# Second MoE in units of 256 tokens with four banks per layer, maxima turned by TensorE, weight sums in the first MoE's last span

## The chip, the cores and the metric

The program runs on one core of one Trainium2 chip. The metric is the device time of one execution in microseconds (us). Five engines matter: PE (TensorE matmul, with PEld its weight loads), DVE (VectorE), ACT (ScalarE), POOL (GpSimd) and SP (SyncE), which issues most DMAs. Accumulators live in PSUM, which the kernel uses as eight banks of 128 x 512 f32; everything else on the chip is in SBUF.

## The reference, cut to what matters

```python
def reference(q, k, v, s, moe_w_in, moe_w_out, moe2_w_in, moe2_w_out):
    a = _attn_ref(q, k, v, s)              # 4 batches, 8 heads, 576 tokens, 64 per head
    x = a.transpose(0, 2, 1, 3).reshape(2304, 512)
    x = _moe_ref(x, moe_w_in, moe_w_out)
    return _moe2_ref(x, moe2_w_in, moe2_w_out)

def _moe_ref(x, w_in, w_out):              # first MoE
    h = x @ w_in                           # 2304 x 512 by 512 x 2048
    sp = np.where(h > 20.0, h, np.log1p(np.exp(np.minimum(h, 20.0))))
    return (h * np.tanh(sp)) @ w_out       # 2304 x 2048 by 2048 x 512

def _moe2_ref(x, w_in, w_out):             # second MoE
    h = x @ w_in
    return (h * (1.0 / (1.0 + np.exp(-1.702 * h)))) @ w_out
```

## The kernel before

Every f32 product is made from three matmuls: each operand is split into a high and a low part, and `mm3` issues high by high, high by low and low by high into one accumulator (three code lines, L593 to L595). The program has three stages. The first holds the attention and the first layer of the first MoE, and ends with the hidden values in DRAM (`h_d`). The second is the second layer of the first MoE. The third is the second MoE.

**Tokens.** The 2304 tokens are cut into five spans, four of 512 and one of 256. Both later stages go span by span.

**Second layer of the first MoE (the loop over `groups1`, L922 on).** Per span, PE accumulates 16 blocks of 128 hidden rows into the span's accumulators: four banks of `acc` for 512 tokens, two for 256, taken with `bank()` in rotation from two pools of eight banks in all. After each block, `bg_step()` runs one background job: conversion and maxima of the second MoE's weights (`out_pass1`, which leaves the output weights in DRAM as `w2_d`, `in_pass`, `in_split`, and the two scales `out_scale` and `in_scale`). At the end of a span ACT copies the accumulators to SBUF (`x2`, L948), DVE takes maxima of absolute values (L823), they go to DRAM (`x2_d`), and a last reduce (L953) leaves one maximum per partition. `across` then takes the maximum over the 128 partitions: a DMA writes the column to a row in DRAM (`row_d`, L790), a second reads the row back to all partitions (L792), and DVE reduces it (L793). It is called seven times, for five spans and for the two weight scales. Behind it on DVE stand the scale computations (`span_scale`).

**Second MoE.** `prep_x(u)` reads a span's `x2_d` and splits it to f16 (ACT L915, DVE L916). `first2` makes one bank of the first layer (`h`): for a span of 512 it is 12 matmuls of 512 columns, twice for each of eight indices j; for the span of 256 it is 24 matmuls of 256 columns, once per j. The pool `ps_1` has one bank for all of this. ACT takes the sigmoid from the bank (L118), DVE multiplies (`z`, L1007). The second layer has Strassen's form with seven products instead of eight: `combos` builds the four sums of blocks of z on POOL (L1015 to L1018) and splits z and the sums into high and low parts (`gh`, `gl`, L1021, L1022); `second2` accumulates the seven products (`p`), one bank each (`ps_7`, seven banks). `pend` holds the second-layer work back by a few steps (`LGH = 4`). `finish` evacuates the seven products into the output rows.

**Weight sums.** `out_pass2(j)` makes the seven block sums of the output weights for pair j: two reads of `w2_d` (`w2f`), four POOL subtractions (`w2d`, L970), three ACT copies (`w2h`, L979) and three DVE subtractions (`w2l`, L980). In the program two of the eight calls stand ahead of the second MoE and six in its first span.

**What sets the order.** The kernel is written in a framework with a scheduler that fixes a static order on every engine when the program is built. Each engine runs its list in order, so an instruction that waits holds back all behind it on that engine.

Of the kernel before, what the change touches and what calls it, by code (L numbers as in the profile page):

```python
# [28 lines left out]
LGH = 4  # L29
# [25 lines left out]
def attention_moe_moe_kernel(  # L55
# [34 lines left out]
    row_d = dram.tile([16, 128], F32, name="row_d")  # L90
# [694 lines left out]
    row_n = [0]  # L785
# [49 lines left out]
    def out_scale():  # L835
        amax(gsc[:, 0:1], wom)
        across(gsc[:, 0:1])
# [32 lines left out]
    def in_scale():  # L870
        nc.vector.tensor_reduce(out=gsc[:, 2:3], in_=rk[:, :, 1], axis=mybir.AxisListType.X, op=ALU.max)
        across(gsc[:, 2:3])
# [47 lines left out]

    acc1 = {}
    for i, (u, t0, W, m0, n) in enumerate(groups1):  # L922
# [8 lines left out]
        for j in range(n):  # L931
# [9 lines left out]
            bg_step()  # L941
        if m0 + n == NF:
# [11 lines left out]
            across(spx[:, u, 0:1])  # L954
            if ready[0]:
                span_scale(u)
            else:
                waiting.append(u)
    while bg:
        bg_step()  # L960

    w2o_t = {}

    def out_pass2(j):
        y = wst_b.tile([128, 2, 512], F32, tag="wst", name="w2f", bufs=NRAW)
        for e in range(2):
            nc.sync.dma_start(out=y[:, e, :], in_=w2_d[j + NF // 2 * e])
        d = tmp_pair(F32, "w2d").rearrange("p (s f) -> p s f", s=4)
        b11, b12, b21, b22 = (y[:, e, h * 256:(h + 1) * 256] for e in range(2) for h in range(2))
        sub = lambda o, a, b_: nc.gpsimd.tensor_tensor(out=o, in0=a, in1=b_, op=ALU.subtract)  # L970
        sub(d[:, 0], b12, b11)
        sub(d[:, 2], b22, b12)
        sub(d[:, 1], b22, d[:, 0])
        sub(d[:, 3], d[:, 1], b21)
        th, tl_ = (wb_p.tile([128, 7, 256], F16, tag="w", name=nm) for nm in ("w2h", "w2l"))
        k = gsc[:, 0:1]
        for s0, s1, src in ((0, 1, y[:, 0, 0:256]), (1, 3, y[:, 1, :]), (3, 7, d.rearrange("p s f -> p (s f)"))):
            h, l = (x[:, s0:s1, :].rearrange("p s f -> p (s f)") for x in (th, tl_))
            nc.scalar.activation(out=h, in_=src, func=AF.Copy, scale=k)  # L979
            nc.vector.scalar_tensor_tensor(out=l, in0=src, scalar=k, in1=h, op0=ALU.mult, op1=ALU.subtract)  # L980
        w2o_t[j] = th, tl_
# [4 lines left out]
    ps_1 = enter_b(tc.tile_pool(name="ps_1", bufs=1, space=PSUM, reuse_waits="tile"))  # L986
# [3 lines left out]
    SECOND = ((6, 2, 5), (4, 0, 3), (2, 3, 2), (3, 5, 6))  # L990
    prod = {}
    ev = {}
    pend = []
    NP = NF // 2

    def first2(u, j, W, e, z, sg):
        ps = ps_1.tile([128, 512], F32, tag="h", name="h2")
        ms = [(0, j + NP if e == 0 else j)] if W == 512 else [(0, j + NP), (1, j)]
        x = x16[u]
        for d, m in ms:  # L1000
            o = ps[:, d * W:(d + 1) * W]
            for c in range(KC):
                t = w2t[c, m // 8]
                hi, lo = (t[:, a, m % 8 * 128:m % 8 * 128 + 128] for a in range(2))
                mm3(o, hi, lo, x[:, 0, c, 0:W], x[:, 1, c, 0:W], d == 0 and c == 0, c == KC - 1)
# [3 lines left out]
    def combos(z, hb):  # L1009
        q_ = z[:, 0:4 * hb].rearrange("p (s t) -> p s t", s=4)  # L1010
        a12, a22, a11, a21 = (q_[:, k] for k in range(4))
        st = tmp_pair(F32, "s2")[:, 0:4 * hb]
        sv = st.rearrange("p (s t) -> p s t", s=4)
        tt = nc.gpsimd.tensor_tensor
        tt(out=sv[:, 0], in0=a21, in1=a22, op=ALU.add)  # L1015
        tt(out=sv[:, 2], in0=a11, in1=a21, op=ALU.subtract)
        tt(out=sv[:, 1], in0=sv[:, 0], in1=a11, op=ALU.subtract)
        tt(out=sv[:, 3], in0=a12, in1=sv[:, 1], op=ALU.subtract)  # L1018
        h, l = (wa_p.tile([128, 7 * 256], F16, tag="w", name=nm)[:, 0:7 * hb] for nm in ("gh2", "gl2"))
        for s0, n_, src in ((4 * hb, 3 * hb, z[:, 0:3 * hb]), (0, 4 * hb, st)):  # L1020
            nc.scalar.activation(out=h[:, s0:s0 + n_], in_=src, func=AF.Copy)  # L1021
            nc.vector.tensor_tensor(out=l[:, s0:s0 + n_], in0=src, in1=h[:, s0:s0 + n_], op=ALU.subtract)  # L1022
        return h, l

    def second2(u, j, hb, which, h, l):
        nt = hb // 128
        if j == 0:
            for p, _, _ in which:
                prod[u, p] = ps_7.tile([128, 512], F32, tag=f"p{p}", name=f"p{p}")
        th, tl_ = w2o_t[j]  # L1030
        for p, a, b_ in which:
            for tb in range(nt):
                o = prod[u, p][:, tb * 256:(tb + 1) * 256]
                ts = slice(a * hb + tb * 128, a * hb + (tb + 1) * 128)
                mm3(o, h[:, ts], l[:, ts], th[:, b_], tl_[:, b_], j == 0 and tb == 0, j == NP - 1)

    def finish(u, W, part):
        t0 = spans[u][0]
        nt = W // 256
        n_ = nt * 256  # L1040
        k, nk = spx[:, u, 3:4], spx[:, u, 0:1]
        pv = lambda p: prod[u, p][:, 0:n_].rearrange("p (t f) -> p t f", t=nt)
# [4 lines left out]
        def tmp(nm):  # L1047
            t = mb.tile([128, 512], F32, tag="x2", name=nm, bufs=4)
            return t[:, 0:n_].rearrange("p (t f) -> p t f", t=nt)

        if part == 0:
            ev[u, "lo"], ev[u, "hi"] = lo, hi = [
                wst_b.tile([128, 2, 512], F32, tag="wst", name=nm, bufs=NRAW)[:, 0:nt] for nm in ("olo", "ohi")
            ]
            e1 = tmp("e1")
            nc.scalar.activation(out=e1, in_=pv(0), func=AF.Copy, scale=k)
            add(lo[:, :, 0:256], 1, e1)
            ev[u, "u2"] = tmp("u2")
            add(ev[u, "u2"], 5, e1)
        else:  # L1060
            lo, hi, u2 = (ev.pop((u, x)) for x in ("lo", "hi", "u2"))
            u3, u4 = tmp("u3"), tmp("u4")
            add(u3, 6, u2)
            add(u4, 4, u2)
            add(hi[:, :, 256:512], 4, u3)
            add(lo[:, :, 256:512], 2, u4)
            add(hi[:, :, 0:256], 3, u3, nk)
            for half, o in enumerate((lo, hi)):
                r0 = t0 + half * W // 2
                nc.sync.dma_start(out=out[r0:r0 + W // 2, :].rearrange("(t p) f -> p t f", p=128), in_=o)  # L1070

    def push(u, j, W, z):
        hb = W // 2
        h, l = combos(z, hb)
        for part, which in enumerate((FIRST, SECOND)):
            def go(part=part, which=which):
# [57 lines left out]
```

## Time and profile before

| What | us |
| --- | --- |
| Median of 3 runs (lowest, highest) | 1088.12 (1085.77, 1090.79) |
| The profiled execution, its own time | 1082.65 |
| Its span in the profile | 1080.8 |
| PE busy in the span | 964.4 (89%) |
| DVE, ACT, POOL busy | 686.2, 562.9, 389.2 |
| First MoE's second layer on PE | 452 to 663 |
| Second MoE on PE, first to last matmul | 662.9 to 1075.1 |

Times in the trace count from the start of the span. The profiled execution is 5.47 us below the median of the runs, and 1.85 us of it lie outside its span. Matmuls are pipelined: the listed length of one is longer than the distance from one start to the next, and the distance is what a sequence costs.

### The profile page before, as it was taken

Reading aid. Unit: us, or ns where it says so; the run is one execution under the profiler, and the core shown is the slowest. Engines: PE = TensorE matmul, PEld = TensorE weight load, DVE = VectorE, ACT = ScalarE, POOL = GpSimd, SP = SyncE. Lnnn points to the kernel's source line nnn. Section 1 sums busy time; section 2 is a strip of 40 time slices with the busy share of each in tenths; the row PEclk is TensorE's granted clock in tenths of the full one; section 3 lists DMA queues with packets and bytes.
Section 4 is the critical chain, followed back from the end, with each engine's and each line's share of the span. In section 5 each row is a group of like instructions: output and inputs, shape, how many; then the busy total and the mean of one; then the engine's idle time right before and its main releaser. Section 6 shows DMA issues by size and latency. Waiting matters only on the chain.

```text
span 1080.8 us, 18613 instructions
## 1 busy us (share of the span) xinstructions
PE 964.4 (89%) x7044; PEld 776.8 (72%) x7044; DVE 686.2 (63%) x1266; ACT 562.9 (52%) x1078; POOL 389.2 (36%) x434
## 2 busy tenths in 40 slices
PE   5587799999999999999999986399989999998997
PEld 4476698888888889988887875156656565665686
DVE  5897776575567756999877945535643553463454
ACT  4886777585658863565555545234333423332332
POOL 3454532241223114772211316155332423333343
PEclk7788999999999999999999997599999999999999
DMA  9799997996799898899894656100110010010010
GB/s 238 175 224 265 243 221 160 211 207 175 162 204 206 153 171 262 282 354 317 266 265 149 234 106 136 61 1 1 39 40 1 3 57 2 1 39 1 1 40 20
DMA packets 185865, 153.87 MB, mean 142 GB/s; under 512 B 118896, under 2 KB 154096, under 8 KB 185776
## 3 DMA queue, kind: packets, MB, share of 16 engines
q1 hardware_dynamic: 179744, 135.38, 50.3%
q0 software_dynamic: 6032, 17.31, 6.8%
q8 instruction: 55, 0.90, 0.3%
q14 instruction: 34, 0.28, 0.1%
HBM read 93.86 MB, written 32.58 MB: 117 GB/s over the span
## 4 chain that ended last, share of the span: by engine, by line
PE 31%; DMA 16%; DVE 12%; issue 5%; ACT 4%; POOL 3%; SPq 0%; DVEq 0%; POOLq 0%; ACTq 0%
PE h L593 6%; PE h L594 6%; PE h L595 6%; PE p L595 4%; PE p L593 4%; PE p L594 4%; DMA row_d<-spx 4%; DMA bc<-row_d 3%; DMA row_d<-gsc 2%; DMA wst<-in_moe_w_out_dram 2%; DVE x L916 1%; DVE z L1007 1%; DVE gl L729 1%; DVE wst L812 1%; ACT sg L118 1%
## 5 line engine op out<-in xcount | busy, mean ns | idle before, releaser
L593 PE MATMUL h<-x,w2i 128*128 128x512 f16 (+1 forms) x320 | 116.1, 363 | 46.9 <-DVE z L1007 46.8
L593 PE MATMUL h<-xh,w 128*128 128x256 f32 x448 | 133.7, 303 | 0.8 <-ACT xh L454 0.8
L118 ACT ACTIVATE sg<-h,spx 128x512 f32<-128x512 f32 x72 | 49.2, 683 | 158.8 <-PE h L595 158.7
L595 PE MATMUL h<-xh,w 128*128 128x256 f32 x448 | 130.1, 291 | 1.9 <-POOL w L589 1.8
L594 PE MATMUL h<-xh,w 128*128 128x256 f32 x448 | 131.0, 293 | 0.0
L593 PE MATMUL p<-w2h,gh 128*128 128x256 f16 x504 | 127.5, 273 | 2.5 <-ACT gh L1021 2.5
L594 PE MATMUL p<-w2l,gh 128*128 128x256 f16 x504 | 127.4, 273 | 0.0
L593 PE MATMUL acc<-gh,w 128*128 128x512 f32 (+1 forms) x320 | 119.9, 375 | 4.5 <-ACT gh L727 4.5
L594 PE MATMUL acc<-gl,w 128*128 128x512 f32 (+1 forms) x320 | 120.1, 375 | 3.1 <-DVE gl L729 3.1
L1015 POOL TENSOR_TENSOR s<-z 128x256 f32<-128x256 f32 (+1 forms) x40 | 29.2, 729 | 255.5 <-DVE z L1007 255.5
L595 PE MATMUL acc<-gh,w 128*128 128x512 f32 (+1 forms) x320 | 119.5, 373 | 0.0
L1007 DVE SCALAR_TENSOR_TENSOR z<-h,sg 128x512 f32<-128x512 f32 x72 | 49.6, 689 | 107.7 <-ACT sg L118 107.7
L594 PE MATMUL h<-x,w2i 128*128 128x512 f16 (+1 forms) x320 | 116.2, 363 | 0.0
L595 PE MATMUL h<-x,w2i 128*128 128x512 f16 (+1 forms) x320 | 116.1, 363 | 0.0
L595 PE MATMUL p<-w2h,gl 128*128 128x256 f16 x504 | 107.7, 273 | 2.6 <-DVE gl L1022 2.6
L118 ACT ACTIVATE P<-P,mx 128x128 f32<-128x128 f32 (+4 forms) x144 | 83.4, 580 | 31.6 <-DVE mx L355 30.8
L336 PE MATMUL s<-kw,qw 128*128 128x288 f32 (+4 forms) x384 | 88.6, 343 | 8.9 <-DVE mx L355 4.6
L729 POOL TENSOR_TENSOR gl<-z,gh 128x1024 fp32r<-128x1024 f32 x18 | 49.0, 2725 | 123.1 <-ACT gh L727 69.3
L382 DVE SCALAR_TENSOR_TENSOR hl<-P,hl 128x512 f16<-128x512 f32 (+2 forms) x104 | 71.4, 686 | 32.4 <-ACT hl L381 32.1
L595 PEld LDWEIGHTS h<-xh,w 128*128 128x128 f32 x448 | 88.0, 196 | 2.5 <-POOL w L589 2.4
L593 PEld LDWEIGHTS h<-xh,w 128*128 128x128 f32 x448 | 87.3, 197 | 2.2 <-ACT xh L454 1.2
L594 PEld LDWEIGHTS h<-xh,w 128*128 128x128 f32 x448 | 88.2, 197 | 0.6 <-DVE xh L455 0.4
(151 smaller groups left out, 2445.7 us busy)
## 6 DMA issues: line engine op xcount, KB each, us to landing
h_d<-hs SPq DMA_DIRECT2D x36, 512.0 KB, 5.0
hg<-h_d SPq DMA_DIRECT2D x36, 512.0 KB, 7.1
wst<-in_moe_w_in_dram SPq DMA_DIRECT2D x32, 512.0 KB, 6.0
wst<-in_moe_w_out_dram SPq DMA_DIRECT2D x32, 512.0 KB, 5.4
vl<-in_v_dram SPq DMA_DIRECT2D x12, 384.0 KB, 4.9
cp<-cum_d SPq DMA_DIRECT2D x16, 288.0 KB, 4.8
ck<-cum_d SPq DMA_DIRECT2D x6, 768.0 KB, 7.4
x_d<-x SPq DMA_DIRECT2D x18, 256.0 KB, 6.1
```

The source lines that it names most:

```text
L118: i = nc.scalar.activation(out=out, in_=in_, func=func, **kw)
L336: nc.tensor.matmul(out=o, lhsT=qw[b, i, g][:, hl, w, :], rhs=kw[b, g][:, hl, c0:c1], start=(e == a == w == 0), stop=False, skip_group_chec ...
L382: nc.vector.scalar_tensor_tensor(out=hv[:, 1, 0:wl], in0=x["P"][:, 0:wl], scalar=PSC, in1=hv[:, 0, 0:wl], op0=ALU.mult, op1=ALU.subtract)
L593: nc.tensor.matmul(out=outp, lhsT=hi_w, rhs=hi_x, start=start, stop=False, skip_group_check=True)
L594: nc.tensor.matmul(out=outp, lhsT=hi_w, rhs=lo_x, start=False, stop=False, skip_group_check=True)
L595: nc.tensor.matmul(out=outp, lhsT=lo_w, rhs=hi_x, start=False, stop=stop, skip_group_check=True)
L729: (nc.vector if e == 0 else nc.gpsimd).tensor_tensor(out=gl[e], in0=z, in1=gh[e], op=ALU.subtract)
L812: nc.vector.tensor_scalar(out=zi, in0=zi, scalar1=29, scalar2=None, op0=ALU.logical_shift_right)
L916: nc.vector.scalar_tensor_tensor(out=t[:, 1, c, 0:W], in0=xr[:, c, 0:W], scalar=k, in1=t[:, 0, c, 0:W], op0=ALU.mult, op1=ALU.subtract)
L1007: nc.vector.scalar_tensor_tensor(out=z, in0=ps, scalar=GSC, in1=sg, op0=ALU.mult, op1=ALU.mult)
L1015: tt(out=sv[:, 0], in0=a21, in1=a22, op=ALU.add)
```

## The change

Three things are changed.

1. The second MoE goes in units of U = 256 tokens, nine of them. `first2` always makes 24 matmuls of 256 columns per j. `ps_1` has four banks. The seven products share four banks, two to a bank but for the last (`HOME`). `combos` and the splits work for two j at a time, `LGH` is 8, and `finish` evacuates a unit of 256 tokens with one output DMA. `prep_x` of the next span stands at the second pair of j in the last unit of a span.
2. `across` no longer goes through DRAM. DVE copies the column to 128 x 128 (L788 of the changed code); two steps later (`soon`) PE transposes this into an accumulator bank taken with `bank()` (L792) and DVE reduces it there (L793), and then the scale computations follow.
3. `out_pass2` is called in the first MoE's last span, after each second block, for all eight pairs.

```diff
-LGH = 4
+LGH = 8
-    def across(col):
-        r = row_n[0]
-        row_n[0] += 1
-        nc.sync.dma_start(out=row_d[r:r + 1, :].rearrange("r p -> p r"), in_=col)
+    def across(col, then):
         t = mb.tile([128, 128], F32, tag="bc", name="bc", bufs=2)
-        nc.sync.dma_start(out=t, in_=row_d[r:r + 1, :].to_broadcast([128, 128]))
-        nc.vector.tensor_reduce(out=col, in_=t, axis=mybir.AxisListType.X, op=ALU.max)
+        nc.vector.tensor_copy(t, col.to_broadcast([128, 128]))
+
+        def turn():
+            ps = bank()
+            nc.tensor.transpose(ps[:, 0:128], t, ident)
+            nc.vector.tensor_reduce(out=col, in_=ps[:, 0:128], axis=mybir.AxisListType.X, op=ALU.max)
+            then()
+
+        soon.append([2, turn])
...
             bg_step()
+            soon_step()
+            if u == len(spans) - 1 and m % 2:
+                out_pass2(m // 2)
...
-    ps_1 = enter_b(tc.tile_pool(name="ps_1", bufs=1, space=PSUM, reuse_waits="tile"))
+    ps_1 = enter_b(tc.tile_pool(name="ps_1", bufs=4, space=PSUM, reuse_waits="tile"))
...
+    HOME = {0: (0, 0), 1: (0, 1), 5: (1, 0), 6: (1, 1), 4: (2, 0), 2: (2, 1), 3: (3, 0)}
...
-    def first2(u, j, W, e, z, sg):
+    def first2(u, t0, j, z, sg):
-        ms = [(0, j + NP if e == 0 else j)] if W == 512 else [(0, j + NP), (1, j)]
-        for d, m in ms:
-            o = ps[:, d * W:(d + 1) * W]
+        for d, m in enumerate((j + NP, j)):
+            o = ps[:, d * U:(d + 1) * U]
...
-                prod[u, p] = ps_7.tile([128, 512], F32, tag=f"p{p}", name=f"p{p}")
+            k, r = HOME[p]
+            if j == 0 and (key, k) not in prod:
+                prod[key, k] = ps_7.tile([128, 512], F32, tag=f"p{k}", name=f"p{k}")
+            o = prod[key, k][:, r * 256:(r + 1) * 256]
...
-    out_pass2(0)
-    out_pass2(1)
-    for u, (t0, W) in enumerate(spans):
-        for j in range(NP):
-            if u == 0 and j + 2 < NP:
-                out_pass2(j + 2)
+    for u, (s0, W) in enumerate(spans):
+        for t0 in range(0, W, U):
+            for jp in range(NP // 2):
```

**Where the instructions stand.** On PE in the second span of the first MoE, where the first transpose has gone (`acc` are the span's accumulators, `w` the weights, `bc` the broadcast column, numbers tell tiles apart). Before:

```order
L593 MATMUL acc_7005<-gh_6994,w_6329 128x512
L594 MATMUL acc_7005<-gl_6996,w_6329 128x512
L595 MATMUL acc_7005<-gh_6994,w_6329 128x512
L593 MATMUL acc_7002<-gh_6994,w_6365 128x512
L594 MATMUL acc_7002<-gl_6996,w_6365 128x512
```

The same place in the changed kernel, where the numbers of the tiles are a few lower:

```order
L592 MATMUL acc_7002<-gh_6991,w_6328 128x512
L593 MATMUL acc_7002<-gl_6993,w_6328 128x512
L792 MATMUL acc_7036<-ident_70,bc_6982 128x128
L594 MATMUL acc_7002<-gh_6991,w_6328 128x512
L592 MATMUL acc_6999<-gh_6991,w_6364 128x512
```

The transpose now stands inside the row of accumulating matmuls, with 299 of the stage's 960 ahead of it. The other six have 367, 429, 625, 696, 806 and 960 ahead of them.

On PE at the handover, from the first MoE's last matmuls to the first of the second MoE (`h`, from `x` and the weights `w2i`). Before:

```order
L593 MATMUL acc<-gh,w 128x256
L594 MATMUL acc<-gl,w 128x256
L595 MATMUL acc<-gh,w 128x256
L593 LDWEIGHTS w2i
L593 MATMUL h_8376<-x_8189,w2i 128x512
L594 LDWEIGHTS w2i
L594 MATMUL h_8376<-x_8189,w2i 128x512
```

And in the changed kernel:

```order
L592 MATMUL acc<-gh,w 128x256
L593 MATMUL acc<-gl,w 128x256
L594 MATMUL acc<-gh,w 128x256
L792 MATMUL acc<-ident,bc 128x128
L592 LDWEIGHTS w2i
L592 MATMUL h_8462<-x_8258,w2i 128x256
L593 LDWEIGHTS w2i
L593 MATMUL h_8462<-x_8258,w2i 128x256
```

The last span's transpose stands between the two MoEs, ahead of every matmul of the second.

On DVE at the same handover (`mx` are the span's maxima, `spx` and `gsc` the scales). Before, behind the reduce of the last span's maxima:

```order
L953 TENSOR_REDUCE spx<-mx_8294 128x1
L1007 SCALAR_TENSOR_TENSOR z_8374<-h_8376,sg 128x512
L793 TENSOR_REDUCE spx<-bc 128x1
L879 TENSOR_SCALAR spx<-spx,gsc 128x1
L880 TENSOR_SCALAR spx<-spx 128x1
L881 RECIPROCAL spx<-spx 128x1
L796 TENSOR_SCALAR spx<-spx 128x1
L883 TENSOR_SCALAR spx<-rk,spx 128x4
L884 RECIPROCAL spx<-spx 128x1
L885 TENSOR_TENSOR spx<-spx,gsc 128x1
L980 SCALAR_TENSOR_TENSOR w2l<-w2d,gsc,w2h 128x1024
L1007 SCALAR_TENSOR_TENSOR z_8374<-h_8391,sg 128x512
```

And in the changed kernel:

```order
L952 SCALAR_TENSOR_TENSOR w2l<-w2f,gsc,w2h 128x512
L952 SCALAR_TENSOR_TENSOR w2l<-w2d,gsc,w2h 128x1024
L832 TENSOR_REDUCE mx_8427<-x_8428 128x2
L832 TENSOR_REDUCE mx_8427<-x_8432 128x2
L952 SCALAR_TENSOR_TENSOR w2l<-w2d,gsc,w2h 128x1024
L990 TENSOR_REDUCE spx<-mx_8427 128x1
L788 COPY bc<-spx 128x128
L793 TENSOR_REDUCE spx<-acc 128x1
L892 TENSOR_SCALAR spx<-spx,gsc 128x1
```

The weight sums' last subtractions now stand ahead of the last span's maxima and of the copy that PE's transpose reads.

## Rows read from the trace of the kernel before

**Rows 1.** Windows by stage: ends, length, busy per engine, granted clock, DMA share, GB/s.

```profile
452.00:663.00 211.00, 203.35 (x965) 171.00 (x964) 168.76 (x266) 114.14 (x148) 76.93 (x45) 0.98 0.78 239
663.00:703.20 40.20, 12.31 (x37) 4.44 (x37) 19.23 (x44) 13.81 (x23) 6.90 (x8) 0.62 0.29 68
703.20:1035.50 332.30, 309.32 (x2091) 203.85 (x2090) 155.46 (x164) 114.29 (x147) 125.20 (x143) 1.00 0.04 15
1035.50:1075.10 39.60, 38.48 (x349) 33.56 (x346) 21.37 (x32) 14.14 (x24) 16.09 (x32) 1.00 0.08 28
1075.10:1080.80 5.70, 0.02 (x1) 0.00 (x0) 2.27 (x6) 0.00 (x0) 0.00 (x0) 0.75 0.25 92
```

**Rows 2.** PE's waits from 663 on: who waited for whom, us, times, longest.

```profile
PE h L593 <- DVE z L1007: 46.8, 16, 17.8
```

**Rows 3.** Timeline of PE, second MoE's start: start, length, instruction, idle before it.

```profile
662.92 0.39 PE L593 MATMUL h<-x,w2i 128*128 128x512 f16 x1
...
665.30 0.38 PE L595 MATMUL h<-x,w2i 128*128 128x512 f16 x1
683.44 0.58 PE L593 MATMUL h<-x,w2i 128*128 128x512 f16 x1 [17.75 <-DVE z L1007]
...
688.08 0.63 PE L595 MATMUL h<-x,w2i 128*128 128x512 f16 x1
```

**Rows 4.** Timeline of DVE in the same stretch.

```profile
673.56 0.29 DVE L793 TENSOR_REDUCE spx<-bc 128x1 f32<-128x128 f32 x1 [7.38 <-DMA bc<-row_d]
...
682.70 0.68 DVE L1007 SCALAR_TENSOR_TENSOR z<-h,sg 128x512 f32<-128x512 f32 x1
695.12 0.29 DVE L793 TENSOR_REDUCE spx<-bc 128x1 f32<-128x128 f32 x1 [11.73 <-DMA bc<-row_d]
```

**Rows 5.** Timeline of PE, a span of 512 tokens, then the span of 256.

```profile
807.24 0.38 PE L593 MATMUL h<-x,w2i 128*128 128x512 f16 x1 [1.39 <-DVE z L1007]
...
828.32 0.38 PE L593 MATMUL h<-x,w2i 128*128 128x512 f16 x1 [1.39 <-DVE z L1007]
...
1046.78 0.27 PE L593 MATMUL h<-x,w2i 128*128 128x256 f16 x1
...
1051.69 0.27 PE L593 MATMUL h<-x,w2i 128*128 128x256 f16 x1
```

**Rows 6.** PE's waits from 452 to 663, columns as in rows 2.

```profile
PE acc L593 <- ACT gh L727: 4.5, 1, 4.5
PE acc L594 <- DVE gl L729: 3.1, 3, 2.2
```

**Rows 7.** Windows behind two of those waits, columns as in rows 1.

```profile
574.90:579.30 4.40, 4.34 (x13) 3.38 (x14) 0.60 (x2) 1.06 (x1) 0.00 (x0) 0.64 0.73 124
...
647.80:654.60 6.80, 6.10 (x27) 5.81 (x28) 4.59 (x4) 5.04 (x9) 5.74 (x5) 0.50 0.32 125
```

**Rows 8.** Timelines of PE (stage's 299th matmul) and DVE, first MoE's second span.

```profile
520.34 0.39 PE L595 MATMUL acc<-gh,w 128*128 128x512 f32 x1
...
525.88 0.14 DVE L953 TENSOR_REDUCE spx<-mx 128x1 f32<-128x4 f32 x1
```

**Rows 9.** Timelines of POOL, DVE and ACT: weight sums, and the last span's maxima.

```profile
651.22 5.99 POOL L970 TENSOR_TENSOR w2d<-w2f 128x256 f32<-128x256 f32 x6
...
668.42 0.72 POOL L970 TENSOR_TENSOR w2d<-w2d,w2f 128x256 f32<-128x256 f32 x1
...
664.90 1.28 DVE L980 SCALAR_TENSOR_TENSOR w2l<-w2d,gsc,w2h 128x1024 f16<-128x1024 f32 x1
...
681.32 1.27 DVE L823 TENSOR_REDUCE mx<-x 128x2 f32<-128x512 f32 x2
...
679.04 1.06 ACT L948 ACTIVATE x<-acc 128x512 f32<-128x512 f32 x2
```

**Rows 10.** Timelines of ACT and DVE, the last unit's evacuation: its first and last step.

```profile
1072.45 0.47 ACT L1056 ACTIVATE e<-p,spx 128x256 f32<-128x256 f32 x1 [1.18 <-PE p L595]
...
1077.00 0.47 DVE L1045 SCALAR_TENSOR_TENSOR olo<-p,spx,u 128x256 f32<-128x256 f32 x1
```

More of the change, by code (lines that the diff above doesn't have):

```diff
@@ L919, in prep_x, with out_pass2 @@
         x16[u] = t
+    w2o_t = {}
+    def out_pass2(j):
+        y = wst_b.tile([128, 2, 512], F32, tag="wst", name="w2f", bufs=NRAW)
+        for e in range(2):
+            nc.sync.dma_start(out=y[:, e, :], in_=w2_d[j + NF // 2 * e])
+        d = tmp_pair(F32, "w2d").rearrange("p (s f) -> p s f", s=4)
+        b11, b12, b21, b22 = (y[:, e, h * 256:(h + 1) * 256] for e in range(2) for h in range(2))
+        sub = lambda o, a, b_: nc.gpsimd.tensor_tensor(out=o, in0=a, in1=b_, op=ALU.subtract)
+        sub(d[:, 0], b12, b11)
+        sub(d[:, 2], b22, b12)
+        sub(d[:, 1], b22, d[:, 0])
+        sub(d[:, 3], d[:, 1], b21)
+        th, tl_ = (wb_p.tile([128, 7, 256], F16, tag="w", name=nm) for nm in ("w2h", "w2l"))
+        k = gsc[:, 0:1]
+        for s0, s1, src in ((0, 1, y[:, 0, 0:256]), (1, 3, y[:, 1, :]), (3, 7, d.rearrange("p s f -> p (s f)"))):
+            h, l = (x[:, s0:s1, :].rearrange("p s f -> p (s f)") for x in (th, tl_))
+            nc.scalar.activation(out=h, in_=src, func=AF.Copy, scale=k)
+            nc.vector.scalar_tensor_tensor(out=l, in0=src, scalar=k, in1=h, op0=ALU.mult, op1=ALU.subtract)
+        w2o_t[j] = th, tl_
     acc1 = {}
@@ L953, in attention_moe_moe_kernel @@
             nc.vector.tensor_reduce(out=spx[:, u, 0:1], in_=mx, axis=mybir.AxisListType.X, op=ALU.max)
[L954 to L981, printed above, removed]
+            across(spx[:, u, 0:1], lambda u=u: span_scale(u) if ready[0] else waiting.append(u))
+    while soon:
+        soon_step()
     switch_set("sigmoid_and_others")
@@ L1030, in second2 @@
+    def second2(key, j, which, h, l):
         th, tl_ = w2o_t[j]
         for p, a, b_ in which:
[L1032 to L1040, printed above, removed]
+            k, r = HOME[p]
+            if j == 0 and (key, k) not in prod:
+                prod[key, k] = ps_7.tile([128, 512], F32, tag=f"p{k}", name=f"p{k}")
+                fresh = True
+            else:
+                fresh = False
+            o = prod[key, k][:, r * 256:(r + 1) * 256]
+            mm3(o, h[:, j % 2, a], l[:, j % 2, a], th[:, b_], tl_[:, b_], fresh, j == NP - 1)
@@ L1066, in finish @@
[L1066 to L1076, printed above, removed]
-                second2(u, j, hb, which, h, l)
-                if j == NP - 1:
-                    finish(u, W, part)
-            pend.append(go)
@@ new lines, in finish, with push, go @@
+            add(o[:, 0, 256:512], 2, u4)
+            add(o[:, 1, 0:256], 3, u3, nk)
+            r0 = spans[u][0] + t0
+            nc.sync.dma_start(out=out[r0:r0 + U, :].rearrange("(t p) f -> p t f", p=128), in_=o)
+    def push(u, t0, jp, z):
+        h, l = combos(z)
+        for j in (2 * jp, 2 * jp + 1):
+            for part, which in enumerate((FIRST, SECOND)):
+                def go(part=part, which=which, j=j):
+                    second2((u, t0), j, which, h, l)
+                    if j == NP - 1:
+                        finish(u, t0, part)
+                pend.append(go)
@@ new lines, in attention_moe_moe_kernel @@
+    for u, (s0, W) in enumerate(spans):
+        for t0 in range(0, W, U):
+            for jp in range(NP // 2):
+                if t0 == W - U and jp == 1 and u + 1 < len(spans):
+                    prep_x(u + 1)
+                z = tmp_pair(F32, "z2")
+                sg = tmp_pair(F32, "sg")
+                for e in range(2):
+                    o = slice(e * 512, (e + 1) * 512)
+                    first2(u, t0, 2 * jp + e, z[:, o], sg[:, o])
+                    if e == 1:
+                        push(u, t0, jp, z)
+                    for _ in range(2):
+                        if len(pend) > LGH:
+                            pend.pop(0)()
```

90 lines of the change are left out of this document (41 added, 49 removed).

## The prediction, made before the changed kernel was run

> **What bounds the kernel now.** I read the windows by stage first [rows 1]. In the first MoE's second layer PE is busy 203 of 211 us, and from 703 on 348 of 372, at full clock; no other engine is busy over 80% of a stage. PE sets the end, and only its waits and gaps are to be had. Between, in the 40.2 us from 663 to 703, PE is busy 12.3 at a clock of 0.62. PE's waits name one releaser for nearly all of the second MoE's loss: the product `z` on DVE, 46.8 us in 16 waits [rows 2]. `first2` has one bank, so no matmul of the next `h` can start until ACT and DVE have read the last.
>
> The waits are of two kinds. At the start [rows 3] the first twelve `h` matmuls run, and the thirteenth comes after 17.75 us. DVE's timeline says why [rows 4]: its list holds `z` behind the reduce that waits for `across`'s DMA, which lands at 673.56, and the next `z` stands behind another such reduce, at 695.12 after an idle 11.73. Then, in the steady loop, a wait of 1.39 us comes back every 21.08 us, which is once per two j [rows 5].
>
> **What the matmuls alone need.** Twelve matmuls of 512 columns start 662.92 to 665.30, so one costs 2.38 / 11 = 0.216. In the last span, which has 256 tokens and already the shape of the change (24 `h` and 21 `p` matmuls of 256 columns per j), one j takes 1051.69 - 1046.78 = 4.91, or 0.109 per matmul, without a wait [rows 5]. The second MoE of before has 768 `h` matmuls of 512 columns, 192 of 256, and 1512 `p` of 256: 768 x 0.216 + 1704 x 0.109 = 352. It took 662.9 to 1075.1, 412.2 us. So 60 us are lost.
>
> **Part 1, units of 256 and four banks.** The columns don't change; 192 + 1536 = 1728 `h` matmuls of 256 cost what 768 of 512 did. There are 9 units of 8 j: 72 x 4.91 = **353.5 us** if no gap comes in. Four banks mean that PE can be four `h` groups ahead of `z`, some 10 us of PE work, where `z` takes 0.68 [rows 4] and the sigmoid before it reads the same bank once more. What could fill the gaps again is another engine: DVE is busy 155 of 332 us, ACT 114, POOL 125 in the loop [rows 1], and the same elements in about 310 us leave them near half. At a unit's end the products' banks must be evacuated before the next unit may write them; the last evacuation of before takes 1072.45 to 1077.47, 5.0 us [rows 10]. The static order puts 29 to 48 `h` matmuls of the next unit (3 to 5 us), and the first products, ahead of the ones that need a bank just read, so I cost it at nothing, at most 1 us at each of eight ends.
>
> **Part 2, maxima by transposes.** It takes the DMA waits off DVE, and with them the start's 17.75 and the like, which are in the 60 above. In the first MoE it also takes off most of PE's waits for `gh` and `gl`: 7.6 us [rows 6], plus what the slow clock behind two of them costs: 4.4 us at 0.64 and 6.8 us at 0.50 [rows 7], of which (4.4 x 0.36) + (6.8 x 0.5) = 5 at most is loss, 3.8 as I count the matmuls' spacing. Together **-11.4**.
>
> What it adds is PE instructions that wait, in an ordered list. The first transpose has 299 accumulating matmuls ahead of it. Before, matmul 299 starts at 520.34, and the maximum that the transpose needs is made at 525.88 to 526.02; a copy of 128 x 128 follows [rows 8]. So PE would stand from 520.7 to about 526.6, **6.0 us**, with everything of the span queued behind it, and the clock behind it would be low for some microseconds, as behind the stalls of before: +2.3. The five between it and the last stand where DVE may or may not be done. A second cost goes with them: two transposes of the rotation take banks, so a span's first accumulators fall on banks that the span before has just filled, and PE waits for ACT's copies. The trace doesn't show either. Together they cost 0 from below, and from above twice the first's wait, 12 us; I take 6, the middle, near the stall of 4.5 us by a late ACT in rows 6. Sum of the additions **+14.3** (from 2, if the list has slack, to 20). Net for the first MoE +3 (-9 to +9), so it ends at 666 in place of 663.
>
> **Part 3, weight sums, and the handover.** Before, PE goes from the last `acc` matmul to `h` without a gap. Now the last transpose stands between, so PE waits for: ACT's copy of the accumulators (1.06), DVE's maxima (1.27), a `w2l` subtraction that stands between (1.28), the last reduce and the copy [rows 9]. With `w2h` of the same size as `w2l` on ACT ahead of it that is 6 us, the lower end. The upper end comes from POOL: 32 subtractions at 0.72 are 23 us, but six in a row beside DVE took 5.99, 1.0 each, or 32 us [rows 9], and the second four pairs can be read only when buffers of the first four are free. If the last subtraction comes late, its `w2h` and `w2l` hold ACT and DVE, and the transpose behind them, to about 16 us. I take 10, the middle, since the last span has 32 us of PE work to cover 8 pairs and needs about all of it. In the gap the clock falls: behind the wait of 17.75 eleven spacings took 688.08 - 683.44 = 4.64 in place of 2.38 [rows 3], +2.3. What the moved sums free in the second MoE (POOL and DVE work in its first span) lies off PE's path once the banks are there: 0.
>
> SBUF ports may make this worse. The Trainium skill ("SBUF — State Buffer", Who interferes with whom) says that a DVE instruction with two SBUF inputs contends with a GpSimd instruction that reads SBUF. `w2l` has two, `w2d` reads two. The 1.0 against 0.72 agrees in direction. By the rule, eight pairs in series would be 8 x 2.5 + 32 x 0.72 = 43 us by an estimate from the rows, which would put the gap at 10 to 13; the sum holds without it.
>
> **The sum.** First MoE ends at 666; gap 10 and slow clock 2.3: first full-speed `h` at 678.3; 353.5 of matmuls: 1031.8; the end from last matmul to last byte is 5.7 as before [rows 1]: a span of 1037.5. With 1.85 outside the span the execution would be 1039.4 against the profiled 1082.65, a gain of 43. The median lies 5.47 above the profiled run, so the forecast is 1088.1 - 43 = **1045 us**.
>
> **Rivals.**
> *Everything slips in for free.* The transposes find their operands ready, and the handover takes its lower 6 us. First MoE -9, gap 6: 654 + 6 + 2.3 + 353.5 + 5.7 = 1021.5, median 1029. For it: the list was made by a planner that puts the transposes late on purpose. Against: 520.34 and 525.88 in [rows 8].
> *The waits move into PE's list.* Transposes and bank reuse cost their upper ends, handover 16 and 1 us at each unit's end: 672 + 16 + 2.3 + 361.5 + 5.7 = 1057.5, median 1065. The -9 to +9 and the 6 to 16 hold it.
> *Two products to a bank, slower than before.* With seven banks, a unit's bank was read while others were written. Now four must be read within one evacuation. If a unit's end waits for the whole of it, 5.0 us, and a clock loss of 1.6 as in the first stretch of [rows 7] follows, eight ends cost 8 x 6.6 = 53, and the median is 1098. It decides from 43 / 8 = 5.4 us per end. For it: four banks in place of seven, and evacuations twice as often. Against: the 3 to 5 us of `h` work that the order puts there, and the last evacuation has no PE work beside it at all, so part of its 5.0 is the end's own waiting.
> The Trainium skill ("PSUM — Partial Sum Buffer", Summary: rules for kernel authors) says to target a different bank when PSUM is read while a matmul runs. By that, two products in one bank would tie the reading of one to the writing of the other, which makes this rival's wait possible at each end. No row of this trace has such a pair.
> *The change doesn't do what it says.* Four banks, but the loop still waits for another engine once per two j. A wait of 1.2 us in each of 36 pairs is 43 us, and the time stays at 1088. For it: the 1.39 of [rows 5] is the delay of a chain over ACT and DVE that stays. Against: the last span runs the same chain with 4.91 per j and no wait.
>
> **How the numbers follow.** Forecast around 1045: 0.62. Free: 0.15. Waits in PE's list: 0.14. Two products to a bank: 0.05. No gain: 0.04. About 0.5% (5.4 us) is what a measurement of this kernel can tell from no change, so faster means under 1082.7: the first three and a little of the rest, 0.91; same 0.04; slower 0.05. The range takes in most of the free and the waiting case, with the first MoE's -9 to +9 and the gap's 6 to 16: 1030 to 1066.
>
> **What would show it.** In the changed kernel's profile, PE's waits for `z` are gone and first `h` to last `p` is 354 to 358 us; PE idles some 6 us before the first transpose, and 6 to 16 us before the first `h`, ended by DVE or ACT; no DMA touches `row_d`; `w2d` and `w2l` end before the first `h`; the eight unit ends show no wait over 1 us. I am wrong if the loop's j takes clearly more than 4.91, if a unit's end waits over 5 us, or if the first MoE ends outside 654 to 672.

## The result and the profile after

The changed kernel takes 1045.8 us (median of 4 runs, 1041.14 to 1054.25) where the kernel before, run beside it, takes 1089.03 (1085.77 to 1090.79): a ratio of 0.9615, 95% interval 0.9549 to 0.9681. The forecast was 1045, range 1030 to 1066. The profiled execution took 1045.3 with a span of 1043.5.

PE's stages in the changed kernel: the first MoE's second layer, the handover, the second MoE and the end (columns as in rows 1: ends, length, busy of PE, PEld, DVE, ACT and POOL, granted clock, DMA share, GB/s):

```profile
456.30:667.20 210.90, 201.45 (x970) 169.00 (x968) 190.46 (x297) 124.88 (x162) 88.43 (x56) 0.98 0.72 248
667.20:681.40 14.20, 0.23 (x1) 0.21 (x2) 9.14 (x11) 5.20 (x7) 9.21 (x10) 0.57 0.11 37
681.40:1037.90 356.50, 356.34 (x3241) 318.13 (x3239) 178.18 (x225) 124.35 (x165) 129.84 (x146) 0.99 0.05 17
1037.90:1043.50 5.60, 0.00 (x1) 0.00 (x0) 1.79 (x5) 0.00 (x0) 0.00 (x0) 0.79 0.25 94
```

Beside [rows 1] the second MoE is the part that moved: 356.5 us with PE busy in all but 0.2, where before it took 412.2 from first to last matmul. From its first to its last `acc` matmul the first MoE takes 210.6 us (456.6 to 667.2), as it did before (210.8, 452.2 to 663.1). The handover, where before `h` followed `acc` without a gap, is now 14.2 us in which PE does one transpose.

All of PE's waits behind 452 (waited for: us, times, longest), from two views, one up to 700 and one from 660 on:

```profile
PE acc L792 <- DVE bc L788: 23.4, 4, 14.0
...
PE p L592 <- DVE e L1060: 0.2, 1, 0.2
```

The 46.8 us of waits for `z` in [rows 2] are gone, and so are the 7.6 us for `gh` and `gl` in [rows 6]. What remains is the wait for the operand of four transposes. Of the products' evacuations only the last is waited for, at the very end of the program, for 0.2 us; the eight unit ends cost nothing. The timeline of PE has the four transposes, the first `h` matmul, and two matmuls one j apart in the loop:

```profile
531.55 0.45 PE L792 MATMUL acc<-ident,bc 128*128 128x128 f32 x1 [6.71 <-DVE bc L788]
551.31 0.30 PE L792 MATMUL acc<-ident,bc 128*128 128x128 f32 x1 [1.96 <-DVE bc L788]
566.58 0.30 PE L792 MATMUL acc<-ident,bc 128*128 128x128 f32 x1 [0.74 <-DVE bc L788]
...
681.17 0.45 PE L792 MATMUL acc<-ident,bc 128*128 128x128 f32 x1 [14.01 <-DVE bc L788]
681.41 0.42 PE L592 MATMUL h<-x,w2i 128*128 128x256 f16 x1
...
883.49 0.27 PE L592 MATMUL h<-x,w2i 128*128 128x256 f16 x1
...
888.40 0.27 PE L592 MATMUL h<-x,w2i 128*128 128x256 f16 x1
```

888.40 - 883.49 is 4.91 us, the j of [rows 5]. What makes the 14.01 us is read by going back from the copy `bc` through ACT's and POOL's timelines:

```profile
680.80 0.23 DVE L788 COPY bc<-spx 128x128 f32<-128x128 f32 x1
...
678.24 1.26 DVE L832 TENSOR_REDUCE mx<-x 128x2 f32<-128x512 f32 x2
...
672.65 1.15 ACT L951 ACTIVATE w2h<-w2d,gsc 128x1024 f16<-128x1024 f32 x1 [6.52 <-POOL w2d L942]
...
675.76 1.06 ACT L985 ACTIVATE x<-acc 128x512 f32<-128x512 f32 x2
...
660.53 2.39 POOL L942 TENSOR_TENSOR w2d<-w2f 128x256 f32<-128x256 f32 x2 [3.87 <-DMA w2f<-w_d]
```

PE's last `acc` matmul starts at 666.89. ACT could copy the accumulators at once, but in its list the copies of the weight sums come first, and the first of those left waits 6.52 us for POOL. POOL had stood idle until 660.53 for the read of the fifth pair, which needs the buffer that the first pair had. So the accumulators are copied at 675.76, the maxima follow at 678.24 and the transpose at 681.17.

### The profile page after: what moved, and what is told of

It reads as the page before. It is cut to its first block, busy times and chain, and to the rows that moved or that the text cites. A ratio compares the mean times of both kernels' runs of the same rounds, so it can differ in the third digit from the quotient of the medians.

```text
span 1043.5 us, 20130 instructions
## 1 busy us (share of the span) xinstructions
PE 961.3 (92%) x7819; PEld 854.4 (82%) x7819; DVE 698.2 (67%) x1293; ACT 560.3 (54%) x1074; POOL 390.1 (37%) x418
## 4 chain that ended last, share of the span: by engine, by line
PE 42%; DVE 10%; DMA 6%; issue 4%; ACT 3%; POOL 3%; SPq 0%; DVEq 0%; POOLq 0%; ACTq 0%
PE h L592 7%; PE h L593 7%; PE h L594 7%; PE p L594 5%; PE p L592 5%; PE p L593 5%; POOL w2d L942 2%; DMA wst<-in_moe_w_out_dram 2%; DVE gl L728 1%; DVE wst L822 1%; DMA wst<-in_moe_w_in_dram 1%; ACT gh L726 1%; DMA pt<-hl 1%; DVE wst L821 1%; PE s L335 1%
## 5 line engine op out<-in xcount | busy, mean ns | idle before, releaser
L592 PE MATMUL h<-x,w2i 128*128 128x256 f16 x576 | 158.2, 275 | 0.0
L593 PE MATMUL h<-x,w2i 128*128 128x256 f16 x576 | 158.1, 274 | 0.0
L594 PE MATMUL h<-x,w2i 128*128 128x256 f16 x576 | 158.0, 274 | 0.0
L594 PE MATMUL p<-w2h,gl 128*128 128x256 f16 x504 | 136.1, 273 | 0.0
L593 PE MATMUL p<-w2l,gh 128*128 128x256 f16 x504 | 136.1, 273 | 0.0
L592 PE MATMUL p<-w2h,gh 128*128 128x256 f16 x504 | 133.5, 273 | 0.2 <-DVE e L1060 0.2
L1028 POOL TENSOR_TENSOR s<-z 128x256 f32<-128x256 f32 x36 | 27.4, 761 | 219.7 <-DVE z L1020 219.7
L1036 DVE TENSOR_TENSOR gl<-s,gh 128x1024 f16<-128x1024 f32 x36 | 44.1, 1226 | 70.3 <-ACT gh L1035 70.3
L594 PEld LDWEIGHTS h<-xh,w 128*128 128x128 f32 x448 | 87.9, 196 | 1.3 <-POOL w L588 1.2
L592 PEld LDWEIGHTS h<-xh,w 128*128 128x128 f32 x448 | 86.8, 196 | 2.6 <-ACT xh L453 1.8
```

The lines of the kernel that those rows point to most:

```text
L592: nc.tensor.matmul(out=outp, lhsT=hi_w, rhs=hi_x, start=start, stop=False, skip_group_check=True)
L593: nc.tensor.matmul(out=outp, lhsT=hi_w, rhs=lo_x, start=False, stop=False, skip_group_check=True)
L594: nc.tensor.matmul(out=outp, lhsT=lo_w, rhs=hi_x, start=False, stop=stop, skip_group_check=True)
L1028: tt(out=sv[:, :, 0], in0=a21, in1=a22, op=ALU.add)
L1036: nc.vector.tensor_tensor(out=lo, in0=si, in1=ho, op=ALU.subtract)
```

## The experiments

Twelve kernels were run, each in three rounds beside the kernel before. From each profiled execution the table gives two stretches: the first MoE's second layer (its first to last `acc` matmul), and from there to the end of the last `p` matmul. Behind that comes the same end of 5.5 to 5.8 us in all.

| Kernel | Ratio to before (95% interval) | first MoE | second MoE with handover |
| --- | --- | --- | --- |
| before | 1 | 210.8 | 412.0 |
| changed | 0.9615 (0.9549 to 0.9681) | 210.6 | 370.7 |
| e1 maxima through DRAM | 0.9799 (0.9738 to 0.9859) | 211.0 | 391.5 |
| e2 sums as before | 0.9554 (0.9506 to 0.9602) | 212.3 | 364.4 |
| e3 units alone | 0.9760 (0.9707 to 0.9813) | 211.8 | 385.8 |
| e4 transposes alone | 0.9737 (0.9690 to 0.9785) | 210.1 | 385.0 |
| e5 one bank | 0.9848 (0.9804 to 0.9893) | 210.7 | 402.1 |
| e6 last transpose later | 0.9553 (0.9515 to 0.9591) | 212.6 | 365.9 |
| e7 half the sums | 0.9505 (0.9456 to 0.9554) | 211.4 | 362.0 |
| e8 best | 0.9409 (0.9373 to 0.9444) | 212.1 | 354.5 |
| e9 best, first transposes early | 0.9472 (0.9437 to 0.9507) | 211.7 | 358.2 |
| e10 less DVE work | 0.9408 (0.9378 to 0.9439) | 209.0 | 355.5 |
| e11 one bank, seven products | 0.9829 (0.9786 to 0.9872) | 211.1 | 400.5 |
| e12 two banks | 0.9520 (0.9481 to 0.9559) | 212.6 | 365.0 |

The stage ahead of these two, the same code in all, ended between 449 and 462 us in these profiles. A kernel's own runs lie 5 to 13 us apart, and there is one profile of each, so a difference of a few us is read from the two columns and not from the spans.

### The parts of the change, one undone or one alone (e1 to e4)

e1 puts the DMAs back:

```diff
-        nc.vector.tensor_copy(t, col.to_broadcast([128, 128]))
-        def turn():
-            ...
-        soon.append([2, turn])
+        nc.sync.dma_start(out=row_d[r:r + 1, :].rearrange("r p -> p r"), in_=col)
+        nc.sync.dma_start(out=t, in_=row_d[r:r + 1, :].to_broadcast([128, 128]))
+        nc.vector.tensor_reduce(out=col, in_=t, axis=mybir.AxisListType.X, op=ALU.max)
+        then()
```

> The changed kernel with one part undone: the maxima go through DRAM again (two DMAs and a reduce in DVE's list), units of 256 and sums moved as in the change. Theory (the gain lies in the second MoE's loop and its four banks; the transposes cost in the first MoE what they free): within 8 us of the changed kernel's 1046, that is 1040 to 1054. The first MoE loses its 9.4 us of waits for transposes and gets back waits for gh and gl of 8 to 12 us. At the handover PE runs four banks of h at once from about 668, then waits some 10 to 14 us for z behind the reduce of the last span's DMA. Rival (the transposes are the gain, since 28 us of the start's waits in the kernel before stood behind those DMAs): 1065 or more, PE waiting over 25 us at the handover.

Measured: 1069.0 us, which is the rival's number. The first MoE is as long as ever, as the theory has it, but the handover is not 10 to 14 us. PE, then what it waited for, from e1's timelines of PE, ACT, POOL and DVE:

```profile
689.42 0.37 PE L593 MATMUL h<-x,w2i 128*128 128x256 f16 x1 [26.60 <-ACT x L985]
708.01 0.37 PE L593 MATMUL h<-x,w2i 128*128 128x256 f16 x1 [6.37 <-DVE z L1020]
...
688.80 1.05 ACT L985 ACTIVATE x<-acc 128x512 f32<-128x512 f32 x2
...
673.97 2.09 POOL L942 TENSOR_TENSOR w2d<-w2f 128x256 f32<-128x256 f32 x2 [8.29 <-DMA w2f<-w_d]
...
669.71 0.28 DVE L795 TENSOR_REDUCE spx<-bc 128x1 f32<-128x128 f32 x1 [5.41 <-DMA bc<-row_d]
...
705.48 0.28 DVE L795 TENSOR_REDUCE spx<-bc 128x1 f32<-128x128 f32 x1 [11.07 <-DMA bc<-row_d]
```

The reduce that waits for a DMA now stands in DVE's list among the weight sums (idle 5.41 us before 669.71). They free their buffers later, the reads come later, POOL starts the last four pairs at 673.97 where the changed kernel has 660.53, and ACT's copy of the accumulators slides from 675.76 to 688.80. Only one bank for `h` was free before that; the next group of 24 waited 26.60 us. The theory had overlooked that the banks of the first layer are the accumulators, so PE could not run four groups ahead.

e2 calls the weight sums as the kernel before did:

```diff
-            if u == len(spans) - 1 and m % 2:
-                out_pass2(m // 2)
...
+    out_pass2(0)
+    out_pass2(1)
     for u, (s0, W) in enumerate(spans):
...
+                    if u == 0 and t0 == 0 and 2 * jp + e + 2 < NP:
+                        out_pass2(2 * jp + e + 2)
```

> The changed kernel with out_pass2 called as before (two pairs ahead of the second MoE, six in its first unit), units and transposes as in the change. Theory (the moved sums' last POOL subtractions are what holds ACT's copy, DVE's maxima and so the last transpose, 14.0 us): the handover's wait falls to 5 to 9 us, and the first unit's products wait some 3 to 10 us for w2h and w2l; 1038 to 1048. Rival (moving the sums is worth a share of the gain, because POOL cannot make sums and combos side by side in a loop without gaps): 1055 or more.

Measured: 1041.7 us, as the theory has it. The waits are smaller than it has them, 3.96 us at the last transpose and 2.6 us for the products (a row of PE's timeline, then one of its waits):

```profile
677.89 0.30 PE L792 MATMUL acc<-ident,bc 128*128 128x128 f32 x1 [3.96 <-DVE bc L788]
...
PE p L592 <- ACT gh L1033: 2.6, 1, 2.6
```

So moving the sums gained nothing: the stretch is 6.3 us shorter with them where they were. The first MoE is 1.7 us longer in this profile, and the intervals of the two ratios overlap, so how much the sums cost is less sure.

e3 is e1 and e2 in one, e4 the kernel before with only `across` changed:

> Units of 256 with four banks alone: maxima through DRAM and sums where they were. Theory (nearly all of the gain is this part): 1040 to 1056, loop j at 4.91 us without waits for z, waits only in the first 30 us behind 663. Rival (parts 2 and 3 carry a third of the gain or more): 1060 or more.

> The kernel before with the transposes alone: spans of 512, one bank, sums as before. Theory: the two waits behind DMAs at the start (17.75 and 10.14 us) and their slow clock go, a wait for the last transpose of 6 to 12 us comes, the first MoE stays within 4 us, and the loop keeps its wait of 1.39 us per 21.08 us: 1060 to 1074. Rival (transposes do all): under 1052. Rival (nothing, the waits of the transposes eat what they free): 1084 to 1092.

Measured: 1063.4 and 1060.0 us. For e3 the rival's number came, for e4 the lower edge of the theory's. What PE waits for in e3, and a row of DVE's timeline:

```profile
PE h L593 <- ACT x L983: 12.9, 1, 12.9
PE h L593 <- DVE spx L893: 6.3, 1, 6.3
...
682.14 0.28 DVE L795 TENSOR_REDUCE spx<-bc 128x1 f32<-128x128 f32 x1 [7.44 <-DMA bc<-row_d]
```

The first of the two waits is for ACT's copy of the accumulators, which stands behind weight sums as in e1, and DVE's part of these stands behind the reduce that waits for the DMA. In e4:

```profile
PE h L593 <- DVE z L1020: 20.4, 15, 1.5
```

The wait of 6 to 12 us for the last transpose, which the theory had for e4, did not come: the list has it behind the first twelve `h`, and it finds its operand ready. The two parts take away mostly different losses. The units remove the waits in the loop (20.4 us in e4), and the transposes remove the waits at the start that hang on the DMAs (12.9 + 6.3 us in e3). Each alone is worth 26 to 27 us of the second stretch (412.0 to 385.8 and 385.0), both 47.6 (to e2's 364.4). The gain is not nearly all in the units, as the theory had it.

### How many banks, and two products to a bank (e5, e11, e12)

```diff
-    ps_1 = enter_b(tc.tile_pool(name="ps_1", bufs=4, space=PSUM, reuse_waits="tile"))
+    ps_1 = enter_b(tc.tile_pool(name="ps_1", bufs=1, space=PSUM, reuse_waits="tile"))
```

> The changed kernel with one bank for the first layer in place of four, all else as in the change. Theory (the banks close the loop's gaps): the list on PE alternates 18, 24, 41 and 1 second-layer matmuls between groups of 24 first-layer ones; behind the 1 the next group waits for sigmoid and z, about 1.4 us as in the loop of before, once per four j, so 18 waits: 18 x 1.4 to 18 x 2 = 25 to 36 us more than the changed kernel, 1068 to 1082. Rival (the shape of 24 matmuls of 256 columns closes them, as in the last span of before, which has one bank and no wait): 1042 to 1052.

Measured: 1075.0 us, the theory's number. PE's waits in e5 hold the 18 that were counted in the order:

```profile
PE h L592 <- DVE z L1020: 23.5, 18, 1.5
```

So the shape of 24 matmuls of 256 columns does not close the loop's gaps by itself. e12 has `bufs=2`:

> The changed kernel with two banks for the first layer in place of four. Theory (the chain over ACT and DVE is about 3 us and a group takes 2.6 on PE with 2.3 of second-layer work between, so one bank of lead is enough in the loop): 1043 to 1050, at most 3 us more at the handover, no wait for z after the first unit. Rival (the lead of four banks is needed): 1055 or more.

Measured: 1041.3 us, a little under the theory's range, and no wait for `z` at all. One more bank is enough; the third and fourth earn nothing that shows. The stretch is even 5.7 us shorter than in the changed kernel, chiefly because the list has the first `h` ahead of the last transpose, and their wait for ACT's copy is shorter than the 14.01 us there:

```profile
PE h L592 <- ACT x L985: 9.4, 1, 9.4
```

What the second bank does is not settled by this. It gives PE a lead over `z`, but it also changes the list. In e5 17 of the 18 waits come where only 1 or 3 second-layer matmuls stand between two groups of `h`. In e12 and in the changed kernel 21 stand between most groups, and so they do in the last span of before, which has one bank and no wait [rows 5]. One bank with a list that is even everywhere was not run.

e11 takes e5 and gives each product its own bank:

```diff
-    HOME = {0: (0, 0), 1: (0, 1), 5: (1, 0), 6: (1, 1), 4: (2, 0), 2: (2, 1), 3: (3, 0)}
+    HOME = {p: (p, 0) for p in range(7)}
```

> One bank for the first layer, as in the run before that had it, and seven banks for the seven products in place of four. Theory (two products in a bank cost nothing, since the evacuation is hidden at each unit's end): within 4 us of the kernel with one bank and four, 1071 to 1079. Rival (sharing costs at each of eight unit ends, 1 us or more): 1067 or less.

Measured: 1076.5 us against e5's 1075.0, and 400.5 against 402.1 in the stretch. Sharing a bank costs nothing that can be seen here.

### The handover (e6, e7)

e6 runs the last span's transpose in a first-layer bank, at the second unit:

```diff
-            ps = bank()
+            ps = ps_1.tile([128, 512], F32, tag="h", name="turn") if late[0] else bank()
...
-    while soon:
-        soon_step()
+    late[0] = True
...
+                if u == 0 and t0 == U and jp == 0:
+                    while soon:
+                        soon_step()
```

> The changed kernel with the last span's transpose moved into the second MoE's second unit, in a bank of the first layer; its scale is needed first in the ninth unit. Theory (the transpose only passes on a delay that ACT's late copy of the accumulators makes, 676.8 in the changed kernel's profile, and the first layer's banks are those accumulators): the first 24 or 48 matmuls start at once, and the others still wait until ACT has copied; 5 to 8 us less, 1037 to 1042. Rival (the transpose is the whole of the 14 us): 1028 to 1034.

Measured: 1043.8 us, 0.9553, between the two forecasts; the stretch is 4.8 us shorter, just under the theory's 5 to 8. PE no longer meets a transpose, and waits all the same, at its first `h`:

```profile
681.23 0.37 PE L592 MATMUL h<-x,w2i 128*128 128x256 f16 x1 [10.15 <-ACT x L986]
```

The releaser is ACT's copy of the accumulators. Of the 14.01 us in the changed kernel the transpose and the maxima ahead of it account for about 4; the rest is the late copy. Not even the first group slipped ahead, since its bank was one of those accumulators.

e7 leaves four of the sums in the last span, and makes the other four in the first unit:

```diff
-            if u == len(spans) - 1 and m % 2:
+            if u == len(spans) - 1 and m % 2 and m // 2 < 4:
                 out_pass2(m // 2)
...
+                    if u == 0 and t0 == 0 and 4 + 2 * jp + e < NP:
+                        out_pass2(4 + 2 * jp + e)
```

> The changed kernel with four of the eight weight sums in the first MoE's last span, those whose reads have free buffers from the start, and the other four in the second MoE's first unit. Theory (the second four are read late and hold POOL, then ACT and DVE): the wait of the last transpose falls from 14.0 to 4 to 7 us, and nothing comes back in the first unit: 1035 to 1042. Rival (the wait is the evacuation's own length, and the sums are no part of it): 1044 to 1048.

Measured: 1040.0 us. The wait of the last transpose is 6.03 us, as the theory has it, and the stretch 8.7 us shorter than in the changed kernel:

```profile
677.74 0.45 PE L792 MATMUL acc<-ident,bc 128*128 128x128 f32 x1 [6.03 <-DVE bc L788]
```

### A version that beats both, and what it does not touch (e8 to e10)

e8 has the edits of e6 and e7, and puts the first two transposes 12 blocks later:

```diff
-        soon.append([2, turn])
+        turns[0] += 1
+        soon.append([14 if turns[0] < 3 else 2, turn])
```

> Four sums in the last span and four in the first unit, the last transpose in the second unit, and the first two transposes 12 blocks later in the list. Theory: the handover costs under 5 us, the first MoE loses its waits of 6.7 and 2.0 us: 1024 to 1033. Rival (the waits come back as waits for gh, or for accumulator banks not yet copied): 1038 or more.

Measured: 1027.6 us, a ratio of 0.9409 to before, and by the two ratios 0.9409 / 0.9615 = 0.979 of the changed kernel. The stretch takes 354.5 us, 1.0 more than 72 j of 4.91. The time is the theory's, but only the handover was won. In the first MoE it is the rival's wait that came: the transposes don't wait any more, and this does (PE, and what ACT stood for just ahead of the copy that it waited for):

```profile
557.05 0.80 PE L592 MATMUL acc<-gh,w 128*128 128x512 f32 x1 [10.83 <-ACT x L988]
...
555.77 0.75 ACT L878 ACTIVATE w2i<-wst,rk 128x512 f16<-128x512 f32 x1 [5.07 <-DVE rk L808]
```

e9 is e8 without the edit above:

> The best kernel so far (four sums in the last span, four in the first unit, the last transpose in the second unit) without the later place of the first two transposes. Theory (the later place is worth nothing: PE's wait only moved from the transposes to the accumulators, 10.8 us, since DVE is behind in that stretch): 1024 to 1031, the first MoE 210 to 213 us. Rival (the later place carries a part of the 18 us between the changed kernel and the best): 1034 or more.

Measured: 1035.9 us, outside the theory's 1024 to 1031 and with the rival's number. But the first MoE, where the later place was meant to help, is the same (211.7 against 212.1). 3.7 us lie at the handover, where the first `h` waits for ACT's copy of the accumulators, as it does not in e8; why the place of two early transposes decides this, the profiles don't show:

```profile
671.11 0.27 PE L592 MATMUL h<-x,w2i 128*128 128x256 f16 x1 [2.29 <-ACT x L986]
```

Another 2.3 us lie ahead of the first MoE's second layer, and the rest in the runs' spread.

e10 takes 10.8 us of work from DVE in the stretch in which it is behind:

```diff
-        amax(wom[:, m:m + 1], y)
...
+    nc.gpsimd.memset(wom, 0.12)
```

> The best kernel so far with 16 DVE reduces of 0.68 us, 10.8 us in all, left out: the maxima of the second MoE's output weights, in whose place a constant stands, so the scale is not worked out from the weights. They lie in the stretch of the first MoE in which DVE is busy 90 to 99%. Theory (DVE's backlog of background jobs sets the first MoE's loss, whichever instruction PE waits on): PE's wait of 10.8 us falls to under 4, the first MoE takes 201 to 206 us in place of 211.8, and the time is 1017 to 1023. Rival (the wait is made by the order and the banks, not by DVE's load): the first MoE stays within 2 us of 211.8 and the time at 1025 to 1030.

Measured: 1029.6 us, 0.9408, no different from e8, which is the rival's number. The wait fell from 10.83 to 7.40 us and the first MoE from 212.1 to 209.0, a third of what was taken away; neither the theory's 201 to 206 nor the rival's 2 us came out. In both kernels ACT's copy of the accumulators stands in its list behind copies of `w2i` that wait for DVE's `rk`:

```profile
557.42 2.67 ACT L878 ACTIVATE w2i<-wst,rk 128x512 f16<-128x512 f32 x4 [3.69 <-DVE rk L809]
...
560.62 0.79 PE L592 MATMUL acc<-gh,w 128*128 128x512 f32 x1 [7.40 <-ACT x L988]
```

So DVE's load is at most a part of it: 3.1 us from one profile of each kernel is little more than the 2.5 by which the first MoE differs among the other kernels. That the order in ACT's list has a share is read from these rows and not shown. A list in which the copy comes first was not tried; what the order alone is worth stays open.

## Why the prediction was right, point by point

**The loop: 353.5 us and no gap.** Right. First `h` to last `p` took 356.5, of which 2 to 3 are the slow clock at the start, as the sum had it (353.5 + 2.3 = 355.8). e5 and e12 show that the banks remove the waits, and that two are enough. That it is the lead over `z` which does it, the reason given, is not shown: with a second bank the list also becomes more even, and the last span of before has no wait with one bank.

**Two products to a bank cost nothing.** Right: 0.2 us of waits in the whole program, and e11. The rival that made the kernel slower by 53 us did not come; as counted beforehand, 29 to 48 `h` matmuls of the next unit cover the evacuation. The rule of the Trainium skill that was named beside it ("PSUM — Partial Sum Buffer", Summary: rules for kernel authors) asks for different banks when one is read while matmuls run; the order keeps the two apart here, so no run shows what a breach would cost.

**The first MoE: -11.4 + 14.3 = +3.** It came to 0 (210.8 to 210.6). The removed waits all went. Of the added, the first transpose was sized by [rows 8] at 6.0 and took 6.71. The others, put at 6 between 0 and 12, took 2.7, so this term was set too high. The slow clock behind the waits, counted from the distances between starts, cost some 4.5 us before and 2.5 after. So about 12.2 us went and 11.9 came. What the prediction didn't see is that the first MoE takes 209 to 213 us in all fourteen kernels, whichever instruction PE waits on. That points to one cause behind the waits, but no run sets it apart. DVE has hardly any time to spare in that stretch, as two windows of the changed kernel show (columns as in rows 1; DVE's is the third busy time, and in the 20 us between them it is 17.9):

```profile
496.00:516.00 20.00, 20.00 (x89) 16.46 (x88) 19.76 (x27) 14.18 (x17) 6.08 (x2) 1.00 0.96 329
...
536.00:556.00 20.00, 18.04 (x80) 14.63 (x79) 19.93 (x31) 12.91 (x15) 7.14 (x2) 1.00 0.92 308
```

The DMA engines are as full there (0.96 and 0.92, the last column but one), and ahead of the first transpose ACT's last copy of a span's accumulators waits for a DMA:

```profile
528.41 0.60 ACT L985 ACTIVATE x<-acc 128x512 f32<-128x512 f32 x1 [3.91 <-DMA w_d<-w2y]
```

The copies share four buffers (tag `x2`) with the background job's `w2y`, and the copy waits until the DMA has written one of these to DRAM. e10 leaves room for DVE's load as a part of the cause and speaks against it as the whole. More such buffers, or fewer DMAs in that stretch, were not tried.

**The handover: 10 us.** The mechanism was right and the size too small: 14.2. The term that was mis-sized is the lateness of the second four pairs. POOL waited for their reads until 660.53, and the copy of the accumulators, behind the sums in ACT's list, came 9 us after PE's last `acc` matmul; the prediction took the middle of 6 to 16 where the upper end was due. Its price of 1.0 per subtraction held: the lengths of POOL's 32 sum to 32.1 us, 9 more than at 0.72 each. Between the first, at 639.40, and the end of the last, at 676.57, POOL also stands idle 3.87 us for the late reads and 1.18 us for a `w2l`. The estimate beside it by the Trainium skill ("SBUF — State Buffer", Who interferes with whom), a gap of 10 to 13 from DVE and POOL sharing a port, has the right direction. A subtraction beside DVE's, in POOL's timeline of the changed kernel, takes 1.17 where 0.72 is the time alone [rows 9]:

```profile
666.94 1.17 POOL L942 TENSOR_TENSOR w2d<-w2f,w2d 128x256 f32<-128x256 f32 x1
```

How much of the 14.2 us goes with the slower subtractions and how much with the late reads was not shown by a run; e7 removes both from the handover together.

**What the parts are worth.** The prediction put the DMA waits and the loop into one loss of 60 us and gave it to both parts together. That sum held, and the first experiments' theory, that the units alone were nearly all of it, fell: e3 and e4 give them equal shares of 26 to 27 us. The third part, the moved sums, was given 4 of the gap of 10, whose lower end of 6 is the evacuation, and nothing in return. In e2 the stretch is 6.3 us shorter without it, which agrees in direction.

**The sum.** The median came out within 1 us of the forecast, partly by errors that cancel. The forecast execution was 1039.4 and the profiled one took 1045.3: 4.3 more in the stage ahead of the change (456.6 against 452.2, in no term of the sum), 3 less in the first MoE, 4 more at the handover, 0.7 more in the loop. The median was then taken 5.47 above the profiled run, as it stood before, and it stands 0.5 above; that this made up for the rest was luck.

## What to carry to other kernels

A gap that comes back once per round can be closed by one more bank for the tile that is waited for, and here the second bank did all of it; count first what the list puts between two uses of the bank, since an even list had no gap with one. Look for its room in accumulators that can share a bank. A reduction across partitions that goes through DRAM costs more than its own latency, since every instruction behind the waiting reduce is late too; turned by TensorE it costs only where the list puts the transpose ahead of its operand. Work moved ahead of a handover has to fit ahead of the copies that free the banks: if its inputs come late, it holds the handover, and half of it was worth more there than the whole (e7, 8.7 us in the stretch). Against none of it (e2) half gained 2.4 us, which is not clear of the spread.

## What was not expected of the hardware

After the 14.01 us wait PE ran at the lower of its two clock levels (1.2 of 2.4 GHz) for close to 5 us, as it did behind the wait in [rows 3]. These windows of the changed kernel (columns as in rows 1) show a granted clock of 0.50, then 0.65, then full:

```profile
681.40:684.00 2.60, 2.60 (x14) 1.85 (x13) 1.64 (x10) 0.00 (x0) 0.00 (x0) 0.50 0.01 3
684.00:687.00 3.00, 3.00 (x20) 2.30 (x19) 0.00 (x0) 0.46 (x1) 0.00 (x0) 0.65 0.00 0
687.00:690.00 3.00, 3.00 (x30) 2.70 (x28) 0.81 (x2) 0.91 (x2) 0.00 (x0) 1.00 0.02 5
```

e8 has no wait there and ran the same stretch 1 us above its ideal. Beyond that, the same code ahead of the change ended between 449 and 462 us, which is more than most of the edits studied here are worth.
